# Turning the last chunk's second product round: silu values as weights, a bank and a store per half

## The chip, the cores and the metric

The kernel runs on one core of a Trainium2 chip. The metric is the device time of one execution in microseconds, and runs are compared by their median. Below, PE is the matrix engine (PEld its weight loads), DVE the vector engine, ACT the scalar engine, POOL the general engine, and SP the queue that issues most DMAs. ACTq and SPq are the issuing sides of ACT and SP. An L with a number is a line of the kernel before.

## The reference

```python
def _attn_ref(q, k, v, S1, S2):
    def phi(x):
        a = np.einsum('rd,bhsd->bhsr', S1, x)
        b = np.einsum('rd,bhsd->bhsr', S2, x)
        return np.einsum('bhsi,bhsj->bhsij', a, b).reshape(*x.shape[:-1], r * r)
    q_p, k_p = (phi(q), phi(k))
    kv = np.einsum('bhsf,bhsd->bhfd', k_p, v)
    z = np.sum(k_p, axis=2)
    num = np.einsum('bhsf,bhfd->bhsd', q_p, kv)
    den = np.einsum('bhsf,bhf->bhs', q_p, z)[..., None] + 1e-06
    return num / den

def _moe_ref(x, w_in, w_out, beta):
    h = x @ w_in
    g = h * (1.0 / (1.0 + np.exp(-beta * h)))
    return g @ w_out

def reference(...):
    x = attn_out.transpose(0, 2, 1, 3).reshape(B * S, H * D)
    return _moe_ref(x, ...)
```

q, k and v are 4 batches x 4 heads x 1088 positions x 32; r is 8. The attention output becomes x, 4352 tokens by 128 features. The second part is a feed-forward layer of width 2048: x times w_in, a swish with a beta for each hidden feature, and the result times w_out. The output is 4352 x 128 in f32.

## The kernel before, in words

The attention part produces x transposed, in f16: xT, features on the 128 partitions and tokens along the free axis. The tokens of a batch stand there in another order than in the output: column 32t+s of a batch is the token of position 34s+t (s from 0 to 31, t from 0 to 33). Since w_in is scaled by beta beforehand (winp) and w_out by 1/beta (woutp), the swish becomes a plain Silu.

The feed-forward layer works on chunks of 512 token columns (tok_chk): eight chunks of 512, numbered 0 to 7, and a last one, chunk 8, of 256. The hidden width is cut into 16 units of 128 (j). For each chunk:

- w1 (from L384) makes a wave: with 512 columns it multiplies two units, with the 256 columns of chunk 8 four units, into a PSUM tile of two banks (wave, 128 x 1024). One Silu on ACT (L402) turns this into the f16 tile g. So a full chunk has eight waves and chunk 8 has four.
- w2 (from L358) adds the second product up in one PSUM bank (moeout). For each unit, woutp is the weight (the stationary side) and g is streamed (512 or 256 columns). The result is transposed: output features on partitions, tokens along the free axis.
- After the last unit of a chunk, DVE transposes 32x32 blocks of moeout into the SBUF tile o_sb (L378, a pool tag with two buffers), and store (L341) writes it out. It issues, for each batch that the chunk lies in, four DMAs, one for each group of 32 features; each moves 32 x n pieces of 32 floats, 128 bytes each. All stores go to SP's queue, except that those of chunk 8 alternate between SP and ACT (L382): two 32 KB stores on each.

The order of all of this is written out by hand. SEQ (L938) is a list of names that mixes attention steps with "+" (a w1) and "-" (a w2); after it, rest(3) (L953) runs the remaining w1 calls, with the w2 calls lagging by three waves, and then the w2 calls that are left. Each engine executes its instructions in program order. In the last 10 us only the feed-forward layer is left: PE alternates between w1 of chunk 8 and w2 of chunk 7, and after the last w1 come all four w2 calls of chunk 8, 16 matmuls of 256 columns.

The PSUM tags are wave0 and wave1 (two banks each), two (two banks), one and moeout (one bank each). moeout of chunks 6 and 8 lies in tag one (ALT, L338), the others' in their own tag. Tag two is used by attention steps, the last of which are n3 and its copies X30 and X31.

The lines that the prediction speaks of: L286 multiplies for the broadcast of beta (128 columns with a weight load for each) and L295 copies the result; L731, L749, L777 and L819 are copies out of PSUM; L738 is the numerator of the attention (small matmuls on parts of the array); L555 sums up kv.

Of the kernel before, what the change touches and what calls it, by code (L numbers as in the profile page):

```python
# [9 lines left out]
F32 = mybir.dt.float32  # L10
F16 = mybir.dt.float16
ACTF = mybir.ActivationFunctionType
MUL = mybir.AluOpType.mult

P = 128
# [3 lines left out]
def kernel(  # L19
# [12 lines left out]
    nc = tc.nc  # L32

    B, H, S, D = q.shape
    R = S1.shape[0]
    F = R * R
    NTOK, DM = out.shape
    DFF = moe_w_in.shape[1]
    NJ = DFF // P
    assert DM == H * D == P and D == 32 and R == 8 and S % 32 == 0  # L40

    T = S // 32
# [19 lines left out]
    tok_chk = [(o, min(TCH, NTOK - o)) for o in range(0, NTOK, TCH)]  # L62
# [3 lines left out]
    sbA = ctx.enter_context(tc.tile_pool(name="sbA", bufs=2))  # L66
# [19 lines left out]
    def sb(shape, dtype, name):  # L86
        return const.tile(shape, dtype, tag=name, name=name)

    def cut(t, ap, extra=0):
        return bass.AP(tensor=t.tensor, offset=t.offset + extra, ap=[list(t.ap[0])] + ap)  # L90
# [134 lines left out]
    for n in range(2):  # L225
# [15 lines left out]
        out=bpos[:, 0:1], in_=cut(ident[:NB], [[3, NJ], [1, 2]], 1), op=ADD, axis=AX.XY  # L241
    )
    nc.vector.tensor_reduce(
        out=bpos[:, 1:2], in_=cut(ident[:NB], [[3, NJ]], 2), op=ADD, axis=AX.X
# [3 lines left out]
        out=gj, in_=cut(ident, [[R, H], [32, 4], [1, R]]), op=ADD, axis=AX.XY  # L248
# [3 lines left out]
        out=mk.rearrange("p h i -> p (h i)"), in_=cut(ident, [[1, H * R], [32, 4]]), op=ADD, axis=AX.X  # L252
# [45 lines left out]
    woutp = sb([P, NJ, P], F16, "woutp")  # L298
# [9 lines left out]
    def win_unit(j):  # L308
        i, u = divmod(j, NU)
        assert i in given  # L310
        return cut(winp, [[NU, P]], i * WP + u)
# [4 lines left out]
    scaled = set()  # L316
# [22 lines left out]
    moe = {"ci": 0, "w": 0, "ready": 0, "acc": None, "slot": 1, "todo": []}  # L339

    def store(o_sb, t0, u0, u1, queues):  # L341
        c = t0 + 32 * u0
        while c < t0 + 32 * u1:
            b, r = divmod(c, S)
            n = min(t0 + 32 * u1 - c, S - r) // 32
            u = (c - t0) // 32
            for g4 in range(4):
                queues[g4 % len(queues)].dma_start(  # L348
                    out=bass.AP(
                        tensor=out.tensor,  # L350
                        offset=out.offset + (b * S + r // 32) * DM + 32 * g4,
                        ap=[[T * DM, 32], [DM, n], [1, 32]],
                    ),
                    in_=o_sb[32 * g4 : 32 * g4 + 32, u : u + n, :],
                )
            c += n * 32

    def w2(ci, j0, jn, g):  # L358
        t0, tw = tok_chk[ci]
        if j0 == 0:  # L360
            if ci in ALT:
                moe["acc"] = ps1.tile([P, TCH], F32, tag="one", name="moeout")
            else:
                moe["acc"] = pso.tile([P, TCH], F32, tag="moeout", name="moeout")
        for jj in range(jn):
            j = j0 + jj
            assert j in scaled
            nc.tensor.matmul(  # L368
                out=moe["acc"][:, :tw],
                lhsT=woutp[:, j, :],  # L370
                rhs=g[jj],
                start=(j == 0),
                stop=(j == NJ - 1),
            )
        if j0 + jn == NJ:
            o_sb = sbA.tile([P, TCH // 32, 32], F32, tag="o_sb", name="o_sb")
            nt = tw // 32
            nc.vector.transpose(  # L378
                out=o_sb[:, :nt, :].rearrange("p t d -> p (t d)"), in_=moe["acc"][:, :tw]
            )  # L380
            last = ci == len(tok_chk) - 1
            store(o_sb, t0, 0, nt, [nc.sync, nc.scalar] if last else [nc.sync])  # L382

    def w1():  # L384
        ci = moe["ci"]
        t0, tw = tok_chk[ci]
        per = TCH // tw
        jn = 2 * per
        j0 = moe["w"] * jn
        wv = wave2("wave")  # L390
        for jj in range(jn):
            o = (jj % per) * tw
            nc.tensor.matmul(  # L393
                out=wv[:, jj // per, o : o + tw],
                lhsT=win_unit(j0 + jj),
                rhs=xT[:, t0 : t0 + tw],
                start=True,
                stop=True,
            )
        g = sbG.tile([P, 2, TCH], F16, tag="g", name="g")  # L400
        gw = per * tw
        nc.scalar.activation(out=g[:, :, :gw], in_=wv[:, :, :gw], func=ACTF.Silu)  # L402
        moe["todo"].append(
            (ci, j0, jn, [g[:, jj // per, (jj % per) * tw : (jj % per + 1) * tw] for jj in range(jn)])
        )
        moe["w"] += 1
        if j0 + jn == NJ:
            moe["ci"] += 1
            moe["w"] = 0

    def first():
        if moe["ci"] < len(tok_chk) and sum(tok_chk[moe["ci"]]) <= moe["ready"]:
            w1()

    def second():
        if moe["todo"]:
            w2(*moe["todo"].pop(0))

    def rest(lag):
        while moe["ci"] < len(tok_chk):  # L420
            w1()
            if len(moe["todo"]) > lag:
                second()
        while moe["todo"]:
            second()
# [16 lines left out]
    def wave2(name):  # L442
        n = moe["slot"] = 1 - moe["slot"]
        return psm.tile([P, 2, 512], F32, tag=f"wave{n}", name=name)

    def two(name):
        return ps2.tile([P, 2, 512], F32, tag="two", name=name)

    def one(name):
        return ps1.tile([P, 512], F32, tag="one", name=name)  # L450
# [532 lines left out]
```

## Time and profile before

| | |
|---|---|
| median of three runs | 102.54 us (101.99, 102.54, 102.57) |
| the profiled execution's own time | 102.77 us |
| its span, first to last instruction | 100.7 us |
| granted PE clock, mean over the span | 0.99 |
| Silu on ACT, L402 | 68 instructions, 65.6 us, 1024 ns each |
| matmuls of w1, L393 | 144, 40.1 us |
| matmuls of w2, L368 | 144, 37.7 us |
| transposes of results, L378 | 9, 6.2 us; 718 ns for 512 columns, 450 ns for 256 |
| stores, L348 | 46 on SP, 2 on ACT; issue 0.46 us (median) |
| packets moved by DMA | 23,677, of which 19,377 are under 512 B |

The busy time of an engine is the time in which it executes instructions. Matmuls are pipelined: one has a modelled length of 0.27 us with 256 columns, though the next starts 0.11 us later, so starts say more than lengths. Idle time of an engine is put down to the event that came last before the engine went on. DMA times run from the start of the issuing instruction to the landing of the last piece.

Times inside the execution are counted from the start of the span. The prediction uses starts and lengths that come from windows of the timeline, down to single instructions.

### The profile page before, as it was taken

The numbers are of one execution on the slowest core, as the hardware profiler recorded it, in microseconds if no ns is written. First come the engines' busy times: TensorE is split into PE (matmuls) and PEld (weight loads), VectorE is DVE, ScalarE is ACT, GpSimd is POOL, SyncE is SP. The second block draws the span as 40 slices with busy tenths as digits, with TensorE's granted clock in tenths as the row PEclk, the third lists the DMA queues.
The fourth block names the chain that finished last, engine by engine and source line by source line (L and its number), as shares of the span: only waits on it lengthen the run. The fifth ranks groups of instructions, "written<-read, shape, count | busy, mean of one in ns | idle before, by whom it ended". The sixth has DMA issues, their size and how long they took to land.

```text
span 100.7 us, 2858 instructions
## 1 busy us (share of the span) xinstructions
PE 94.6 (94%) x1173; PEld 45.6 (45%) x1173; DVE 59.8 (59%) x126; ACT 79.3 (79%) x103; POOL 34.7 (34%) x41
## 2 busy tenths in 40 slices
PE   5999988999999999999999999999999999999940
PEld 2425732334365443434654434555534444446720
DVE  4759799897876985687894679569362020020210
ACT  1523758997999979899998699999848999999910
POOL 5228669469239601924990032900000000000000
PEclk9999999999999999999999999999999999999996
DMA  2999999999960680023000230006000415013163
GB/s 52 290 231 279 393 409 358 226 210 254 405 237 14 113 216 7 7 42 62 7 0 3 46 62 0 0 0 108 3 0 13 72 20 97 14 20 55 33 106 50
DMA packets 23677, 11.35 MB, mean 113 GB/s; under 512 B 19377, under 2 KB 21489, under 8 KB 23665
## 3 DMA queue, kind: packets, MB, share of 16 engines
q1 hardware_dynamic: 22880, 11.06, 42.6%
q8 instruction: 9, 0.15, 0.6%
q10 hardware_dynamic: 752, 0.11, 0.6%
q0 software_dynamic: 32, 0.02, 0.2%
q14 instruction: 4, 0.02, 0.1%
HBM read 8.95 MB, written 2.23 MB: 111 GB/s over the span
## 4 chain that ended last, share of the span: by engine, by line
PE 78%; DMA 7%; SPq 3%; ACT 3%; DVE 2%; issue 1%; ACTq 1%; POOL 0%; POOLq 0%
PE wave L393 28%; PE moeout L368 25%; PE kvz L555 5%; PE nps L738 5%; DMA beta_r<-in_moe_beta_dram 4%; DMA out_dram<-o_sb 3%; PE kps L457 3%; SPq L348 3%; PE kvz L196 2%; PE qps L457 2%; DVE o_sb L378 2%; PE cps L695 2%; PE aps L531 1%; PE betaps L286 1%; PE dps L610 1%
## 5 line engine op out<-in xcount | busy, mean ns | idle before, releaser
L402 ACT ACTIVATE g<-wave 128x1024 f16<-128x1024 f32 x68 | 65.6, 1024 | 6.7 <-PE wave L393 6.0
L393 PE MATMUL wave<-xT,winp 128*128 128x512 f16 (+1 forms) x144 | 40.1, 369 | 0.2 <-PE aps L531 0.2
L368 PE MATMUL moeout<-g,woutp 128*128 128x512 f16 (+1 forms) x144 | 37.7, 367 | 0.3 <-ACT g L402 0.3
L393 PEld LDWEIGHTS <-winp 128*128 128x128 f16 x144 | 15.1, 115 | 15.7 <-issue 3.1
L368 PEld LDWEIGHTS <-woutp 128*128 128x128 f16 x144 | 13.6, 98 | 15.3 <-issue 2.7
L378 DVE STREAM_TRANSPOSE o_sb<-moeout 128x512 f32<-128x512 f32 (+1 forms) x9 | 6.2, 687 | 21.5 <-PE moeout L368 14.5
L507 POOL TENSOR_TENSOR kp<-kab 128x512 f32<-128x512 f32 (+2 forms) x11 | 12.4, 1156 | 9.2 <-DVE kab L486 7.1
L507 POOL TENSOR_TENSOR qo<-qab 128x512 f32<-128x512 f32 (+1 forms) x10 | 12.0, 1227 | 7.1 <-DVE qab L718 7.1
L518 DVE STREAM_TRANSPOSE qt<-qo 128x512 f32<-128x512 f32 (+1 forms) x12 | 8.7, 756 | 2.1 <-POOL qo L507 1.9
L196 PE MATMUL kvz<-idle 128*128 128x448 f16 x22 | 7.6, 478 | 1.1 <-DVE idle L99 1.1
L306 POOL TENSOR_TENSOR winp<-w_in_sb,beta_bc 128x512 f16<-128x512 f32 x4 | 5.2, 1320 | 1.9 <-DMA w_in_sb<-in_moe_w_in_dram 1.7
L555 PE MATMUL kvz<-kp,v 128*32 128x64 f32 x288 | 5.3, 221 | 0.0
L429 DVE STREAM_TRANSPOSE kT<-k 128x1088 f32<-128x1088 f32 (+2 forms) x5 | 5.2, 1049 | 0.0
L435 DVE STREAM_TRANSPOSE qT<-q 128x1088 f32<-128x1088 f32 (+2 forms) x5 | 5.2, 1049 | 0.0
L709 POOL TENSOR_TENSOR ct<-ct,qab 128x288 f32<-128x288 f32 x2 | 2.2, 1108 | 8.8 <-DVE ct L705 8.8
L555 PEld LDWEIGHTS kvz<-kp,v 128*32 128x32 f32 x288 | 4.3, 110 | 1.8 <-issue 1.2
L486 DVE STREAM_TRANSPOSE kab<-kps 128x288 f32<-128x288 f32 x8 | 3.3, 456 | 2.8 <-PE kps L457 2.8
L738 PE MATMUL nps<-qt,nd 32*32 32x288 f32 x192 | 4.8, 413 | 0.0
L320 ACT ACTIVATE woutp<-w_out_sb,rbeta 128x128 f16<-128x128 f32 x14 | 4.6, 398 | 0.0
L196 PEld LDWEIGHTS <-idle 128*128 128x128 f16 x22 | 2.6, 125 | 4.5 <-issue 2.9
L507 DVE TENSOR_TENSOR kp<-kab 128x512 f32<-128x512 f32 (+1 forms) x5 | 4.5, 920 | 0.0
L749 DVE CAST xT<-nps 128x576 f16<-128x576 f32 x3 | 2.3, 758 | 2.5 <-PE nps L738 2.3
(94 smaller groups left out, 70.5 us busy)
## 6 DMA issues: line engine op xcount, KB each, us to landing
v<-in_v_dram SPq DMA_DIRECT2D x15, 144.0 KB, 6.1
k<-in_k_dram SPq DMA_DIRECT2D x3, 544.0 KB, 6.4
q<-in_q_dram SPq DMA_DIRECT2D x3, 544.0 KB, 7.8
out_dram<-o_sb SPq DMA_DIRECT2D x20, 64.0 KB, 1.9
w_out_sb<-in_moe_w_out_dram SPq DMA_DIRECT2D x2, 512.0 KB, 7.6
w_in_sb<-in_moe_w_in_dram SPq DMA_DIRECT2D x2, 256.0 KB, 5.2
w_in_sb<-in_moe_w_in_dram SPq DMA_DIRECT2D x1, 512.0 KB, 6.9
k<-in_k_dram SPq DMA_DIRECT2D x1, 288.0 KB, 3.0
```

The costliest lines, as they stand in the source:

```text
L196: nc.tensor.matmul(out=kvz0[:, F:], lhsT=idle, rhs=cut(idle, [[0, 7], [1, F]]), start=fresh, stop=True, skip_group_check=True,)
L306: eng.tensor_tensor(out=winp[:, c], in0=w_in_sb[:, c], in1=beta_bc[:, c], op=MUL)
L368: nc.tensor.matmul(out=moe["acc"][:, :tw], lhsT=woutp[:, j, :], rhs=g[jj], start=(j == 0), stop=(j == NJ - 1),)
L378: nc.vector.transpose(out=o_sb[:, :nt, :].rearrange("p t d -> p (t d)"), in_=moe["acc"][:, :tw])
L393: nc.tensor.matmul(out=wv[:, jj // per, o : o + tw], lhsT=win_unit(j0 + jj), rhs=xT[:, t0 : t0 + tw], start=True, stop=True,)
L402: nc.scalar.activation(out=g[:, :, :gw], in_=wv[:, :, :gw], func=ACTF.Silu)
L429: nc.vector.transpose(out=kT2[b % 2][:, t0:t1].rearrange("p t s -> p (t s)"), in_=k_t[b][:, t0:t1].rearrange("p t d -> p (t d)"),)
L435: nc.vector.transpose(out=qT2[b % 2][:, t0:t1].rearrange("p t s -> p (t s)"), in_=q_t[b][:, t0:t1].rearrange("p t d -> p (t d)"),)
L507: (eng or nc.vector).tensor_tensor(out=cut(dst[b][:, j0:j1], [[F, n], [R, R], [1, R]]), in0=left, in1=cut(a0, [[R, n], [0, R], [1, R]], NJ ...
L518: nc.vector.transpose(out=QT[b][:, j0:j1].rearrange("p j h c s -> p (j h c s)"), in_=QO[b][:, j0:j1].rearrange("p j h f -> p (j h f)"),)
L555: nc.tensor.matmul(out=KVZ[b][32 * h : 32 * h + 32, :F], lhsT=v_t[b][:, h, j, :], rhs=KP[b][:, j, h, :], start=(j == 0), stop=(j == NJK - ...
L738: nc.tensor.matmul(out=tiles[g // 2][32 * h : 32 * h + 32, g % 2, :JW], lhsT=ND[b][rows, fc, 32 * h : 32 * h + 32], rhs=QT[b][rows, :, h, ...
```

## The change

For chunk 8 alone, the second product is turned round: g is the weight and woutp is streamed, so the result comes out with tokens on the partitions and the 128 output features along the free axis. The 256 tokens are two halves of 128, each with a PSUM bank of its own (tag one and the first bank of tag two). In each w2 call, four units are multiplied for half 0 and then the same four for half 1, in all 32 matmuls of 128 columns with 32 weight loads. After the last unit of a half, DVE copies its bank to a new tile o_tm (128 x 128), and one DMA of 64 KB stores it: half 0 from ACT, half 1 from SP. The partitions of o_tm must come in the order of the rows in DRAM, so that four neighbouring rows (2 KB) are written from four partitions; for this the Silu of chunk 8 reads the wave in order and writes column 32u+s of each block of 128 to place 4s+u (u from 0 to 3). The Silus of the other chunks are as before, and their stores too.

```diff
+    def w2_turned(ci, j0, jn, g):
+        t0, tw = tok_chk[ci]
+        assert tw == 2 * P
+        if j0 == 0:
+            moe["acc"] = [one("moeout"), two("moeout")[:, 0]]
+        for hf in range(2):
+            acc = moe["acc"][hf][:, :P]
+            for jj in range(jn):
+                j = j0 + jj
+                assert j in scaled
+                nc.tensor.matmul(
+                    out=acc,
+                    lhsT=g[jj][:, P * hf : P * hf + P],
+                    rhs=woutp[:, j, :],
+                    start=(j == 0),
+                    stop=(j == NJ - 1),
+                )
+            if j0 + jn == NJ:
+                b, r = divmod(t0 + P * hf, S)
+                o_sb = sbA.tile([P, P], F32, tag="o_tm", name="o_tm")
+                nc.vector.tensor_copy(out=o_sb, in_=acc)
+                (nc.scalar, nc.sync)[hf].dma_start(
+                    out=bass.AP(
+                        tensor=out.tensor,
+                        offset=out.offset + (b * S + r // 32) * DM,
+                        ap=[[T * DM, 32], [DM, 4], [1, DM]],
+                    ),
+                    in_=o_sb,
+                )
+
     def w2(ci, j0, jn, g):
         t0, tw = tok_chk[ci]
+        if ci == len(tok_chk) - 1:
+            return w2_turned(ci, j0, jn, g)
...
-            last = ci == len(tok_chk) - 1
-            store(o_sb, t0, 0, nt, [nc.sync, nc.scalar] if last else [nc.sync])
+            store(o_sb, t0, 0, nt, [nc.sync])
...
         g = sbG.tile([P, 2, TCH], F16, tag="g", name="g")
         gw = per * tw
-        nc.scalar.activation(out=g[:, :, :gw], in_=wv[:, :, :gw], func=ACTF.Silu)
+        if ci == len(tok_chk) - 1:
+            n = 2 * gw // P
+            nc.scalar.activation(
+                out=cut(g, [[P, n], [1, 4], [4, 32]]),
+                in_=cut(wv, [[P, n], [32, 4], [1, 32]]),
+                func=ACTF.Silu,
+            )
+        else:
+            nc.scalar.activation(out=g[:, :, :gw], in_=wv[:, :, :gw], func=ACTF.Silu)
```

## The prediction

> **What bounds the kernel now.** The page's first lines are read first, to see which engines could set the end.
>
> ```profile
> span 100.7 us, 2858 instructions
> ## 1 busy us (share of the span) xinstructions
> PE 94.6 (94%) x1173; PEld 45.6 (45%) x1173; DVE 59.8 (59%) x126; ACT 79.3 (79%) x103; POOL 34.7 (34%) x41
> ```
>
> These are averages over stages. The change touches only the last chunk, so the chain of waits from 93 us on is read next (start, length, what).
>
> ```profile
> 92.69 1.67 DMA out_dram<-o_sb
> 94.36 0.01 issue
> 94.37 0.73 DVE o_sb L378
> 95.10 0.02 issue
> 95.12 1.58 DMA out_dram<-o_sb
> 96.70 0.44 DVE o_sb L378
> ```
>
> The chain blames stores for the two transposes (DVE, L378). That is a coincidence of times: tile o_sb has two buffers, so the transpose at 96.69 needs the stores of two chunks earlier, whose last issue (92.69) landed after 1.67, at 94.36. The store issued at 95.12 belongs to chunk 7. The true releaser is in the timeline:
>
> ```profile
> 92.23 3.77 ACT L402 ACTIVATE g<-wave 128x1024 f16<-128x1024 f32 x4 [0.21 <-PE wave L393]
> ...
> 94.55 1.82 PEld L368 LDWEIGHTS <-woutp 128*128 128x128 f16 x16
> 94.65 2.00 PE L368 MATMUL moeout<-g,woutp 128*128 128x256 f16 x16
> 96.69 0.45 DVE L378 STREAM_TRANSPOSE o_sb<-moeout 128x256 f32<-128x256 f32 x1 [1.60 <-DMA out_dram<-o_sb]
> 97.17 0.91 ACTq L348 DMA_DIRECT2D out_dram<-o_sb  x2
> ```
>
> Four Silus run gapless, about 0.90 apart, to 96.00. Narrower windows put the last four matmuls at 96.05 to 96.38 (start of the last), the transpose at 96.69, 0.31 after that start. It ends at 97.14; SP and ACT each issue two stores, the last on SP at 97.65. A window on it gives 1.9 to landing: 99.53. The span ends at 100.66, so 1.1 of closing barriers follow. So here: Silu, four matmuls, transpose, two issues in a row, one landing. Only what moves 99.53 counts.
>
> **The change, part by part.**
>
> *Matmuls.* 16 of 256 columns become 32 of 128 columns, each with a weight load of its own, from g instead of woutp. The nearest row is the beta product, also 128 columns with new weights each time:
>
> ```profile
> 10.59 0.22 PEld L286 LDWEIGHTS <-bsel 48*128 48x128 bf16 x4 [0.20 <-issue]
> 10.59 0.39 PE L286 MATMUL betaps<-bq,bsel 48*128 48x128 bf16 x4
> ...
> 11.02 0.59 ACT L295 COPY beta_bc<-betaps 128x512 f32<-128x512 f32 x1
> ```
>
> One such matmul has a modelled length of 0.216, so three steps take 0.39-0.216, 57 ns each; single starts show 56 in the steady part. The old steps are 109 ns apart (single starts again): 16 are 1.74, 32 new ones of 56 are 1.79, equal work. The 24 pairs of the first three waves run from 94.65 to 96.00 (24x0.056=1.34; before, 12x0.109=1.31 plus a short wait), just when the last Silu ends. What changes is the wait: old weights were loaded ahead, now the load itself waits for the Silu (behind it on PE are only the eight last pairs). I charge one step, 0.06: starts at 96.11 (first), 96.28 (fourth, end of half 0), 96.50 (eighth, half 1). Nothing (0) and a whole load (0.10, mean of L368's loads) bound it.
>
> The row is short (four pairs, 48 rows of weights). [...] Without it: no long 128-column run is in this trace, but 63 small matmuls at L738 pass in 1.53 (24 ns a pair), so issuing alone does not hold a pair above 56, and I keep 56.
>
> *Copies in place of the transpose.* The beta row gives 0.25 from the start of the last 128-column matmul (10.77) to its reader (11.02). Half 0's copy starts at 96.53, while half 1 is multiplied. Its length: DVE copies of 256 columns (L731) take 0.385 to 0.424, the transposes grow by 0.267 per 256 columns (450 to 717 ns), so 128 columns cost 0.385-0.133=0.25 (bounds 0.20 and 0.385). Half 0 ends at 96.78, half 1, ready at 96.75, queues behind it and ends at 97.03 instead of 97.14. Two tiles o_tm of their own, so no store is waited for.
>
> *Stores.* Four of 32 KB in 128-byte pieces become two of 64 KB in 512-byte pieces: 1,024 packets become 256. One issue per queue disappears. ACT issues half 0 at 96.81; nothing stands behind it on ACT. SP still has chunk 7's four stores first, the last at 96.56 for 0.51, to 97.07; with the gap before a next issue half 1 goes at about 97.15, not with its data at 97.06. So 0.09 of the path before it is cover, and the issue that used to stand at 97.65 is gone. Landings by size:
>
> ```profile
> out_dram<-o_sb SPq DMA_DIRECT2D x20, 64.0 KB, 1.9
> ...
> out_dram<-o_sb SPq DMA_DIRECT2D x4, 16.0 KB, 1.5
> ...
> out_dram<-o_sb SPq DMA_DIRECT2D x2, 32.0 KB, 1.8
> out_dram<-o_sb ACTq DMA_DIRECT2D x2, 32.0 KB, 1.7
> ```
>
> The 16 KB row has the same 128 packets as the new store, the 64 KB row the same bytes in 512. Packets of 128 B take 11.5 ns, the 512 B ones of beta_r 27; with 8 per DMA engine that adds 0.12 to 1.53. I take 1.65, nearer to the row with the same packet count, with 1.4 (fastest 16 KB store) and 1.9 as ends. Half 1 lands at 98.80, half 0 at 98.46, chunk 7's last at 96.56+1.92=98.48: half 1 is last.
>
> *Silu written in row order.* The reads stay contiguous; each f16 goes 8 bytes from the one before, in 32 runs of 32. It is on the path four times (waves of chunk 8), and no row shows an ACT write like it. For the cut into runs:
>
> ```profile
> L295 ACT COPY beta_bc<-betaps 128x512 f32<-128x512 f32 x4 | 2.4, 588 | 0.8 <-PE betaps L286 0.8
> ...
> L819 ACT COPY kvd<-kvz 128x256 f32<-128x256 f32 x1 | 0.4, 376 | 0.0
> L777 ACT COPY kvd<-kvz 128x128 f32<-128x128 f32 x1 | 0.3, 265 | 1.0 <-PE kvz L196 1.0
> ```
>
> 588-265 over 384 elements is 0.841 ns each, so 256 should take 373; L819, which reads runs of 32, takes 376. 8 runs cost 3 ns, 32 runs 12, four Silus 0.05, less than the 0.09 of cover. For the stride: weight loads from winp read every fourth f16 and take 113 to 115 ns against 98 from woutp, 15% more. 15% of 0.90 is 0.14, four times 0.54: the near upper bound; a second cycle per element, 1024x0.841=0.86 each, is the far one. A gain is excluded, since the element rate stays. [...]
>
> *The PSUM bank* of half 1 (tag two) was last read by the x30/X30 copies at about 75 us: nothing. 32 more PE entries make no further instruction load: the ninth 16 KB one came after some 2,240 PE entries, they are some 250 apart, and the new total is 2,403.
>
> Sum: 99.53-98.80=0.73 less. Own execution 102.77 (span 100.66 and 2.1 around it): 102.04. The median of the runs is 0.23 below that execution: 102.54-0.73=101.81.
>
> **The rivals** (times by the median).
> - *Shorter landing.* If 512-byte pieces cost what 128-byte ones do, half 1 lands at 97.15+1.4=98.55, just behind chunk 7's at 98.48: gain 0.98, 101.6.
> - *PE becomes the bound.* If weight loads are not hidden, a step is as long as one of L368's, 98 ns: the 24 pairs end at 97.00, the last matmul starts at 94.65+0.10+31x0.098=97.79, its reader at 98.04, copy to 98.29, issue at 98.32, landing at 99.97: 0.44 later than now, 103.0. It decides from 56 ns on, where the 24 pairs outlast the Silu; steps between give times between. For it: the row has four pairs only. Against: L738, and the same load is hidden in that row. [...]
> - *A strided write at the price of the strided weight load.* 0.54-0.09 later: gain 0.28, 102.3.
> - *A strided write at half rate*, the other side: 4x0.86-0.09=3.35 later, less 0.73: 105.2. Place: the four Silus of chunk 8, which run gapless, so all of it is exposed. From 0.21 extra per Silu the gain is gone, from 0.46 the kernel is over 1% slower. For it: no ACT row writes with a stride. Against: every ACT row has one rate for f32 and f16 outputs.
> - *A store beside an instruction load.* Some stores land after 3 to 4.2 (maximum of the o_sb tile). If half 1 did, at 100.15 to 101.35: 103.2 to 104.4. Against: the count of PE entries above.
> - *Nothing moves*, if the last landing is set by chunk 7 or by barriers: excluded, since chunk 7 lands 1.05 earlier than the end of now.
>
> **How the numbers follow.** 1% is 1.03 us, about what a measurement of this kernel can tell from no change (its three runs span 0.58). Forecast 0.60; shorter landing 0.11; PE bound 0.09; strided write at 15% 0.09; half rate 0.08; late store 0.03. Faster by over 1% needs 101.5 or less: half of the shorter-landing case and the fast edge of the forecast with the spread of runs, 0.17. Slower: half rate, late store and a little of the PE case's far end, 0.12. Same: 0.71. The range goes from 101.4 (shorter landing, a fast run) to 102.6 (the 15% case, or a landing of 1.9 at 102.1, with the spread of runs); half rate, late stores, the far half of the PE case and the edges are left out, together 0.2.
>
> **What would show it.** After: Silus of chunk 8 still 1.02 to 1.05 and 0.90 apart; 128-column steps of 56 ns; two DVE copies of about 0.25; one ACT issue near 96.8 and one SP issue near 97.15, landing in 1.65. Silus of 1.2 or more, steps of 80, or a landing of 1.9 or more would name the term that fails.

## The result, and the profile after

The changed kernel takes 107.16 us (median of 107.02 to 107.47), the kernel before 102.48 in the same comparison: a ratio of 1.047, 95% interval 1.043 to 1.051. It is 4.7 us slower; 101.8 was forecast. The profiled execution's span went from 100.7 to 105.3.

The page after: span and busy times, then the groups of Silus (line, engine, operation, shapes, count, busy time, mean ns of one, idle time before).

```profile
span 105.3 us, 2884 instructions
...
PE 94.9 (90%) x1189; PEld 45.8 (43%) x1189; DVE 59.9 (57%) x127; ACT 84.8 (81%) x103; POOL 34.7 (33%) x41
...
L441 ACT ACTIVATE g<-wave 128x1024 f16<-128x1024 f32 x64 | 61.9, 1024 | 6.6 <-PE wave L424 5.8
...
L435 ACT ACTIVATE g<-wave 128x1024 f16<-128x1024 f32 x4 | 9.3, 2510 | 0.2 <-PE wave L424 0.2
```

ACT is the only engine that got clearly busier: 84.8 against 79.3. All of that is in one row. The 64 Silus that write in order still take 1024 ns; the four of chunk 8 take 2510 ns for the same 1024 elements.

The end of the timeline after:

```profile
92.02 9.28 ACT L435 ACTIVATE g<-wave 128x1024 f16<-128x1024 f32 x4 [0.21 <-PE wave L424]
...
94.52 0.60 PE L424 MATMUL wave<-xT,winp 128*128 128x256 f16 x4 [1.29 <-ACT g L435]
...
97.23 1.06 PE L368 MATMUL moeout<-woutp,g 128*128 128x128 f16 x16
...
99.09 0.62 PE L368 MATMUL moeout<-woutp,g 128*128 128x128 f16 x8 [0.81 <-ACT g L435]
...
101.36 0.62 PE L368 MATMUL moeout<-woutp,g 128*128 128x128 f16 x8 [1.65 <-ACT g L435]
101.79 0.52 DVE L378 COPY o_tm<-moeout 128x128 f32<-128x128 f32 x2 [5.49 <-PE moeout L368]
102.11 0.65 ACTq L379 DMA_DIRECT2D out_dram<-o_tm  x1
102.33 0.65 SPq L379 DMA_DIRECT2D out_dram<-o_tm  x1
```

The four Silus run gapless for 9.28, where they took 3.77; they start 0.21 earlier in this execution, so the last one ends 5.3 later (101.30 against 96.00). PE now waits for ACT ahead of the third wave and the last two w2 calls (the bracketed idle times of 1.29, 0.81 and 1.65), and ahead of the fourth wave too (1.25). In the kernel before, PE is busy without a gap from 92 to 96 (4.00 of 4.00). Behind the last Silu things are faster: its end to the last landing (102.33+2.06=104.39) is 3.09, where it was 3.53. And 1.13 of closing barriers became 0.89. 5.3-0.44-0.24 is the 4.6 of the span.

So the account is one large loss on ACT and a small gain behind it. Open were: is the price the write's stride, the cut into runs of 32, or a disturbance by the turned product? And why is the gain 0.44 rather than 0.73?

### The profile page after: what moved, and what is told of

It reads as the page before. It is cut to its first block, busy times and chain, and to the rows that moved or that the text cites. A ratio compares the mean times of both kernels' runs of the same rounds, so it can differ in the third digit from the quotient of the medians.

```text
span 105.3 us, 2884 instructions
## 1 busy us (share of the span) xinstructions
PE 94.9 (90%) x1189; PEld 45.8 (43%) x1189; DVE 59.9 (57%) x127; ACT 84.8 (81%) x103; POOL 34.7 (33%) x41
## 4 chain that ended last, share of the span: by engine, by line
PE 82%; ACT 6%; issue 5%; DVE 4%; ACTq 0%
PE wave L424 29%; PE moeout L400 26%; PE kvz L196 6%; ACT g L435 5%; PE kvz L594 5%; PE nps L777 4%; PE kps L496 3%; PE qps L496 2%; PE cps L734 2%; PE aps L570 1%; PE dps L649 1%; DVE woutp L331 1%; ACT g L441 1%; PE gp L607 1%; DVE xT L693 1%
## 5 line engine op out<-in xcount | busy, mean ns | idle before, releaser
L441 ACT ACTIVATE g<-wave 128x1024 f16<-128x1024 f32 x64 | 61.9, 1024 | 6.6 <-PE wave L424 5.8
L400 PE MATMUL moeout<-g,woutp 128*128 128x512 f16 x128 | 35.7, 379 | 0.2 <-ACT g L441 0.2
L400 PEld LDWEIGHTS <-woutp 128*128 128x128 f16 x128 | 12.1, 98 | 15.0 <-issue 2.7
L410 DVE STREAM_TRANSPOSE o_sb<-moeout 128x512 f32<-128x512 f32 x8 | 5.7, 717 | 21.4 <-PE moeout L400 21.3
L435 ACT ACTIVATE g<-wave 128x1024 f16<-128x1024 f32 x4 | 9.3, 2510 | 0.2 <-PE wave L424 0.2
```

The lines of the kernel that those rows point to most:

```text
L400: nc.tensor.matmul(out=moe["acc"][:, :tw], lhsT=woutp[:, j, :], rhs=g[jj], start=(j == 0), stop=(j == NJ - 1),)
L410: nc.vector.transpose(out=o_sb[:, :nt, :].rearrange("p t d -> p (t d)"), in_=moe["acc"][:, :tw])
L435: nc.scalar.activation(out=cut(g, [[P, n], [1, 4], [4, 32]]), in_=cut(wv, [[P, n], [32, 4], [1, 32]]), func=ACTF.Silu,)
```

## The experiments

### The Silu in order, the rest of the change kept

```diff
-                out=cut(g, [[P, n], [1, 4], [4, 32]]),
+                out=cut(g, [[P, n], [32, 4], [1, 32]]),
```

> The changed kernel, but the four Silus of chunk 8 write in order; the stores are the same, so the last 256 tokens go to other output rows. Theory 1 (the strided write is what costs): Silus back at 1.02 us, the last one ends 5.5 us earlier; the tail from its end to the last landing stays 3.1 us against 3.5 before, so about 0.4 us faster than before, 102.0. Theory 2 (g as weights, or the turned product, disturbs ACT or SBUF): Silus stay near 2.5 us, about 107.

Measured: 101.47 us, ratio 0.989 (0.983 to 0.996). The row of the four Silus on its page:

```profile
L435 ACT ACTIVATE g<-wave 128x1024 f16<-128x1024 f32 x4 | 3.8, 1028 | 0.2 <-PE wave L424 0.2
```

The Silus are back at 1.03 (four in 3.77), and with weights loaded from g, two banks, two copies and two stores all in place the kernel is about 1% faster than before. Theory 2 falls: nothing in the turned product disturbs ACT.

### The strided write alone, in the kernel before

```diff
-        nc.scalar.activation(out=g[:, :, :gw], in_=wv[:, :, :gw], func=ACTF.Silu)
+        if ci == len(tok_chk) - 1:
+            n = 2 * gw // P
+            nc.scalar.activation(
+                out=cut(g, [[P, n], [1, 4], [4, 32]]),
+                in_=cut(wv, [[P, n], [32, 4], [1, 32]]),
+                func=ACTF.Silu,
+            )
+        else:
+            nc.scalar.activation(out=g[:, :, :gw], in_=wv[:, :, :gw], func=ACTF.Silu)
```

> The kernel before, with only the strided write of the Silu in chunk 8 (so the tokens of each block of 128 come out in another order). Theory 1: Silus of 2.5 us, the last one 5.5 us later, 108. Theory 2: Silus of 1.02 us, 102.5.

Measured: 107.81 us in one execution, beside 102.52. The groups of its last 18 us:

```profile
L404 ACT ACTIVATE g<-wave 128x1024 f16<-128x1024 f32 x4 | 9.3, 2511 | 0.2 <-PE wave L393 0.2
...
L410 ACT ACTIVATE g<-wave 128x1024 f16<-128x1024 f32 x4 | 3.9, 1026 | 0.2 <-PE wave L393 0.2
```

L404 is the strided Silu, L410 the one in order: 2511 ns without any other part of the change. The two experiments together make up the result: +5.3 for the strided write (one execution) and for the rest -1.0 (the run above) or -0.6 (the version below that reads out of order), against +4.7 for both.

### What in the write costs

The kernel before, followed by 13 Silus and three DVE copies of the last wave (128x1024 from PSUM) that write to scratch places. `parts(s)` cuts each block of 128 into s runs whose neighbours lie s elements apart, as the change does with s=4.

```diff
     rest(3)
...
+    def parts(s):
+        return [[P, 8], [1, s], [s, P // s]]
...
+    silu(cut(scr, [[1, 1024]]), straight)
+    for s in (2, 4, 8, 16, 32):
+        silu(cut(scr, parts(s)), cut(wv, [[P, 8], [P // s, s], [1, P // s]]))
+    silu(cut(scr, [[2, 1024]]), straight)
+    silu(cut(scr, [[4, 1024]]), straight)
+    silu(cut(scr, [[32, 4], [P, 8], [1, 32]]), cut(wv, [[256, 4], [32, 8], [1, 32]]))
+    silu(cut(beta_bc, [[1, 1024]]), straight)
+    silu(cut(beta_bc, [[2, 1024]]), straight)
+    silu(cut(beta_bc, parts(4)), cut(wv, [[P, 8], [32, 4], [1, 32]]))
+    silu(cut(scr, [[P, 8], [4, 32], [1, 4]]), cut(wv, [[P, 8], [1, 32], [32, 4]]))
+    for o in ([[1, 1024]], [[2, 1024]], [[4, 1024]]):
+        nc.vector.tensor_copy(out=cut(xT, o), in_=straight)
```

> The kernel before, followed by 13 Silus and 3 DVE copies of 128x1024 from PSUM that write at different strides; the time has 13 more Silus in it and is not compared. Theory 1a (each 2-byte write that does not join its neighbour costs): f16 at strides 2, 4, 8, 16, 32 all near 2.5 us, f32 at stride 2 near 1.0. Theory 1b (distance in bytes costs): price grows with the stride, f16 at stride 2 cheaper than 2.5, f32 at stride 2 (8 bytes) like f16 at stride 4. Theory 3 (the cut into runs of 32 costs, not the stride): long runs at stride 2 and 4 at 1.0 us, runs of 32 in order at other places 2.5 us. DVE: 1.2 us at every stride if the price is ACT's own, longer at stride 2 and 4 if it is SBUF's.

Narrow windows of its timeline, one for each instruction, in the order of the diff (L960 holds all 13 Silus, L977 the DVE copies; scr is f16, beta_bc f32; start, length). The line at 125.25 reads the wave every 128 bytes and writes in order, the one at 120.37 writes runs of 32 in order at other places:

```profile
97.89 1.02 ACT L960 ACTIVATE scr<-wave 128x1024 f16<-128x1024 f32 x1 [2.12 <-DVE o_sb L378]
...
98.95 1.30 ACT L960 ACTIVATE scr<-wave 128x1024 f16<-128x1024 f32 x1
...
100.28 2.43 ACT L960 ACTIVATE scr<-wave 128x1024 f16<-128x1024 f32 x1
...
102.75 4.69 ACT L960 ACTIVATE scr<-wave 128x1024 f16<-128x1024 f32 x1
...
117.91 2.43 ACT L960 ACTIVATE scr<-wave 128x1024 f16<-128x1024 f32 x1
...
120.37 1.02 ACT L960 ACTIVATE scr<-wave 128x1024 f16<-128x1024 f32 x1
...
122.40 1.07 ACT L960 ACTIVATE beta_bc<-wave 128x1024 f32<-128x1024 f32 x1
...
123.50 1.96 ACT L960 ACTIVATE beta_bc<-wave 128x1024 f32<-128x1024 f32 x1
...
125.25 1.06 ACT L960 ACTIVATE scr<-wave 128x1024 f16<-128x1024 f32 x1
...
128.93 2.42 DVE L977 CAST xT<-wave 128x1024 f16<-128x1024 f32 x1
```

All of them together, lengths in us:

| write | in order | every 2nd | every 4th | every 8th | every 16th | every 32nd |
|---|---|---|---|---|---|---|
| ACT, f16 | 1.02 | 1.30 | 2.43 | 4.69 | 4.44 | 4.60 |
| ACT, f32 | 1.02 | 1.07 | 1.96 | | | |
| DVE, f16 | 1.22 | 1.29 | 2.42 | | | |

- One long run at every 4th place takes 2.43, exactly as 32 runs do. Runs of 32 in order at other places take 1.02. So the cut is free (theory 3 falls), as the row of L819 had it for a read; it was only the wrong row to price the stride by.
- The price grows with the distance up to 16 bytes (f16 every 8th, 4.69) and then stays (4.44 and 4.60): theory 1b, with a ceiling. But bytes are not all of it: at 8 bytes an f32 write costs 1.07, an f16 write 2.43, where theory 1b had them alike. Theory 1a, one price for any 2-byte write that stands alone, falls with the 1.30. So none of the theories fits the whole table.
- DVE pays the same 2.42 for f16 at every 4th place. So the price is not ACT's own. Where it arises was not tried.

### The row order made on the read side

```diff
-                out=cut(g, [[P, n], [1, 4], [4, 32]]),
-                in_=cut(wv, [[P, n], [32, 4], [1, 32]]),
+                out=cut(g, [[P, n], [4, 32], [1, 4]]),
+                in_=cut(wv, [[P, n], [1, 32], [32, 4]]),
```

> The changed kernel, with the row order made on the read side: the Silu reads the wave in PSUM every 32nd f32 (128 bytes apart) and writes f16 in order. Theory 1, if the price belongs to writes alone: Silus at 1.02 us and 102.0 in all, as without any reordering. If a stride costs the same on the read side, or more since it is wider: Silus of 2.5 us or more, 107 or more. Theory 2: 107.

Measured: 101.88 us (ten runs, 101.45 to 102.17), ratio 0.994 (0.991 to 0.997). This version writes the same output as the changed kernel. It is 0.6% faster than the kernel before, little but outside the interval of no change, and 5% faster than the changed kernel. Its timeline:

```profile
92.26 3.77 ACT L435 ACTIVATE g<-wave 128x1024 f16<-128x1024 f32 x4 [0.21 <-PE wave L424]
...
94.68 2.02 PE L368 MATMUL moeout<-woutp,g 128*128 128x128 f16 x32
96.52 0.52 DVE L378 COPY o_tm<-moeout 128x128 f32<-128x128 f32 x2 [1.40 <-PE moeout L368]
96.85 0.65 ACTq L379 DMA_DIRECT2D out_dram<-o_tm  x1
97.19 0.65 SPq L379 DMA_DIRECT2D out_dram<-o_tm  x1
```

Reading PSUM every 128 bytes (in groups of four) costs ACT nothing here: 3.77 for four, the same as in the kernel before. The start of the last Silu to the last landing takes 4.21 (94.99 to 99.20), as in the version without any reordering (94.41 to 98.62), where it was 4.57 before (94.96 to 99.53). So the two differ in nothing that the change touches, and the 0.4 between their medians is no cost of the read; their intervals overlap. The profiled executions differ ahead of the change already: the first Silu of chunk 8 starts at 91.69 without reordering, at 92.26 here and at 92.23 in the kernel before.

### The row order made in DRAM addresses, and four stores per half

Both with Silus in order. The first lists the target rows as 4 groups of 32, the second issues one DMA for each group:

```diff
-                        ap=[[T * DM, 32], [DM, 4], [1, DM]],
+                        ap=[[DM, 4], [T * DM, 32], [1, DM]],
```

> The changed kernel with Silus that write in order and one store per half whose target side lists the rows as 4 groups of 32 (the row order is made in DRAM addresses; each piece is still 512 bytes). If only the number of pieces counts, the store lands about 2.0 us after its issue as with the read-side order, 101.9 in all. If the shape decides how many DMA engines share the pieces (4 groups: 4 engines with 32 pieces each, 32x0.027=0.86 against 0.22), it lands about 0.6 us later, 102.5, no gain left.

Measured: 102.98 us beside 102.41, ratio 1.006 (1.004 to 1.009). SP's store is issued at 96.72 and its last piece lands 3.08 later, at 99.81; the issue on ACT alone takes 1.14. The landing of SP's store is signalled in five steps, where a store of 32 by 4 rows has 16. Its 128 pieces of 28 ns take 0.96 from the first to the last, 3.8 at a time on average; in the read-side version 128 pieces of 27 ns take 0.35, 10 at a time. While the two stores move, the DMA share is 0.2 to 0.3 of the 16 engines; with the plain target below it is 0.6 to 0.9. From 3.8 at a time the estimate is four DMA engines in place of 16; the trace does not name the engine of a piece, so it was not shown. The shape takes back all of the gain and a little more.

```diff
-                (nc.scalar, nc.sync)[hf].dma_start(
+                for u in range(4):
+                    (nc.scalar, nc.sync)[hf].dma_start(
...
-                        offset=out.offset + (b * S + r // 32) * DM,
-                        ap=[[T * DM, 32], [DM, 4], [1, DM]],
+                            offset=out.offset + (b * S + r // 32 + u) * DM,
+                            ap=[[T * DM, 32], [1, DM]],
...
-                    in_=o_sb,
+                        in_=o_sb[32 * u : 32 * u + 32],
```

> The same, but each half is stored by four DMAs of 32 partitions and 16 KB, half 0 all on ACT, half 1 all on SP. If a landing is set by the bytes and pieces of its own DMA, each issue takes 0.43 and each lands within 1.5 to 1.6, but the last issue on SP stands 3x0.47 later, at about 98.6, landing near 100.2: about 1.0 us slower than the read-side order, 102.9. If the long issue (0.65 against 0.43) belongs to 512-byte pieces, each of the four takes 0.65 and the last lands near 101.

Measured: 102.96 us in one execution (13 of the kernel before took 101.84 to 102.90), and the last landing at 99.92. Size and landing of its stores:

```profile
out_dram<-o_tm ACTq DMA_DIRECT2D x4, 16.0 KB, 1.6
out_dram<-o_tm SPq DMA_DIRECT2D x4, 16.0 KB, 1.5
```

The landings are short, and the issues between 0.32 and 0.44, so the long issue does not belong to 512-byte pieces as such (here 32 in each store). On ACT the four issues run in a row, 0.40 to 0.47 apart, and the last store lands 3.66 behind the end of the last Silu (99.21 and 95.55); in the read-side version the last landing of all stands 3.17 behind it. On SP the last issue stands at 98.55, near the forecast 98.6, but by luck: its third and fourth issue start at 98.01 and 98.55, each 0.02 after the landing of one of ACT's stores with the same semaphore (98.00 and 98.53), so SP waited for those landings, and not only for its own issues. What four stores cost without these waits was not run.

### The same store with a plain target

The read-side version, with each half going to 128 neighbouring rows (other rows than the reference's):

```diff
-                        offset=out.offset + (b * S + r // 32) * DM,
-                        ap=[[T * DM, 32], [DM, 4], [1, DM]],
+                        offset=out.offset + (t0 + P * hf) * DM,
+                        ap=[[DM, P], [1, DM]],
```

> The read-side order, but each half goes to 128 neighbouring rows of the output, so both sides of the store are plain (other rows than the reference's; the stores have to wait for earlier ones to the same rows, so the time is not compared, only issue and landing of the two stores). If the 0.65 us issue and the 2.0 us landing come from the row pattern of the target, they fall to about 0.43 and 1.65; if they come from 128 pieces of 512 bytes, they stay.

The issues are 0.35 each, against 0.65 of the read-side version. Sizes and landings here:

```profile
out_dram<-o_tm SPq DMA_DIRECT2D x1, 64.0 KB, 1.6
out_dram<-o_tm ACTq DMA_DIRECT2D x1, 64.0 KB, 1.8
```

and in the changed kernel:

```profile
out_dram<-o_tm ACTq DMA_DIRECT2D x1, 64.0 KB, 2.0
out_dram<-o_tm SPq DMA_DIRECT2D x1, 64.0 KB, 2.1
```

The same 128 pieces of 512 bytes land in 1.65 on SP (1.78 on ACT) when both sides are plain, and in 2.0 to 2.1 when the target has a pattern of 32 by 4 rows. The stores of chunk 7 are not the reason: in the changed kernel the last of them lands at 99.67, long before its own two are issued. The landing counts from the start of the issue, and the issue is longer by 0.30; from the end of SP's issue the landing takes 1.30 here, 1.35 in the read-side version and 1.41 in the changed kernel. So most of the difference is the issue itself, and together it is the 0.37 that the forecast gain lacked. The rows of a plain target also lie side by side, those of the other in groups of four, 34 rows apart; whether the pattern or this distance counts was not separated.

## Why the prediction was wrong

**The step that failed** is the stride of the Silu. The prediction priced the strided write by the row of a cut, which put the four Silus at 0.05 in all, and not by the 15% of the strided weight load; that the stride itself is free on ACT was the author's estimate, which no row showed. They cost 5.3 at their end: 2.51 instead of 1.02 each, and 2.25 from start to start (92.02 to 98.78 for three) instead of 0.91. The row chosen was a read cut into runs, and it told the truth about cuts. No row told of a strided write, and for that very reason the range should have stayed open on this side. The rival "a strided write at half rate" had the mechanism, the place and the sign. Its price, 0.86 per Silu, was still too low: the extra is 1.49 in length and 1.34 in spacing, 1.3 to 1.5 ns for each of the 1024 elements where one further slot was priced at 0.841. It was given 0.08. The bound of 15% from winp's weight loads was no bound either.

**What was right.** The rest of the change makes the kernel faster: the read-side version, which is the change without the strided write, takes 101.88, where 101.81 was forecast. Its steps, each against its term:

| step | forecast | read-side version |
|---|---|---|
| spacing of 128-column matmuls with a weight load each | 0.056 | 0.056 over 24 in a row, (95.97-94.68)/23 |
| reader behind the last matmul of half 0, after the last Silu's end | 0.53 | 0.49 |
| length of a copy of 128 columns | 0.25 | 0.29 |
| half 1's copy ends, after the last Silu's end | 1.03 | 1.01 |
| SP's issue, held up by chunk 7's stores | 97.15 | 97.19 |
| issue to landing of half 1 | 1.65 | 2.01 |
| gain from the last Silu's start to the last landing | 0.73 | 0.36 |

The one term of these that was clearly mis-sized is the landing, 0.36 too short. The sum of pieces came out for a plain target on SP (1.65 measured); the longer issue of the row pattern was not in it. That 101.88 stands so near 101.81 is luck in part. The prediction held the closing barriers fixed ("Only what moves 99.53 counts"), but from the last landing to the end of the span they take 0.89 in this version and 1.13 in the kernel before. The 0.36 and this 0.24 make up nearly all of the 0.64 between the medians (0.35 to 0.95 by the interval). Why the barriers are shorter was not tried; with the strided write alone, where the stores are those of the kernel before, they take 1.01.

**PE as the bound** did not come: pairs of a weight load and a 128-column matmul stand 56 ns apart over 24 in a row, and 58 over all 32 with the pause for the last Silu in it. The beta row of four pairs, with its 57 (56 in single starts), had the right figure. No store met a 16 KB instruction load: the changed kernel still has nine of them, and the ninth starts at 85.07, long before the two stores (102.11 and 102.33).

## What to carry to other kernels

When ACT has to change an order on the way from PSUM to SBUF, let it read out of order and write in order: here it read PSUM every 128 bytes (in groups of four) at full rate, 1.03 for each Silu, and wrote f16 every 8 bytes at 0.4 of it, 2.51. If no row of the profile shows the kind of access that a change introduces, on the side where it introduces it, the cost is unknown and need not be small; multiply the far bound by how often it stands on the path before choosing the near one. For a store, price the shape of the target as well as bytes and pieces: 32 by 4 rows took 0.36 longer to land than 128 plain ones (2.01 against 1.65), and 4 by 32 rows another 1.1 (3.08).

## What the runs showed of the hardware that was not expected

- A strided f16 write to SBUF costs ACT and DVE nearly the same time (2.43 and 2.42 at every 4th place); on ACT it has a ceiling of 4.4 to 4.7 from every 8th place on. An f32 write at the same 8 bytes costs 1.07.
- The issue of one store on SP takes 0.35 with a plain target, 0.65 with 32 by 4 rows, and 0.69 (on ACT 1.14) with 4 by 32 rows.
- In the profiled execution of the changed kernel the granted clock stayed at 1.00 through 9.3 us in which PE was busy for only 4.36. With the strided write alone and nearly the same waits of PE for ACT it fell to 0.50 from 98 to 100, and the matmuls of w2 there stand 213 ns apart in place of 109; the last Silu, which ends at 101.41, hides it. So such waits can go with a lower clock; what decides it was not tried.
